# Splitting product 3 into seven small products in layers 0 to 4 of a cross network, with three of four state sums moved to accumulating DMAs

## The chip, the cores and the metric

The kernel runs on one core of a Trainium2 chip. The metric is the time of the device for one launch, in microseconds (us). A core has TensorE (PE in the profile; PEld are its weight loads, which overlap the products), VectorE (DVE), ScalarE (ACT), GpSimd (POOL), SyncE (SP, which here only starts DMAs) and 16 DMA engines that all queues share.

## The reference

```python
# x0: 16384 x 1024, ws: 6 x 1024 x 1024, bs: 6 x 1024, all bf16
x = x0
for l in range(6):
    proj = einsum('bd,de->be', x, ws[l]) + bs[l]
    x = x0 * proj + x
return x
```

## The kernel before, in words

The batch is cut into 16 pairs of 2 x 512 rows. A pair's state is held turned, features on the partitions: a tile `[128, 2, 8, 512]` with the two batch halves n and eight blocks of features. One pair in one layer is a 1024 x 1024 weight times 1024 rows, which Strassen's scheme (Winograd's form) makes of seven products of 512 x 512 by 512 rows, each 16 matmuls of 128 x 128 by 512. On the right sides of the products stand quarters of the state (products 1, 2 and 3) or differences of them made by VectorE: T13 (for products 5 and 7, one operation of 4096 elements a partition), T2 (product 6) and T4 (product 4). On the left stand quarters of the weight or combinations of them. ScalarE evicts the results from the accumulators (`ev`, with the bias where a sum is done, and `evi` for the small ones) into tiles P1s, P5s, S53, U2s and C2 (its pool is `cb`), and VectorE adds them up, multiplies by x0 and adds the state.

A product can itself be split once more: seven small products of 256 x 256 by 256 rows (`inner`, four matmuls of 128 x 128 by 256 each, line 429), in place of 16 matmuls in `mm` (line 421). This takes combined weights (`combo(l, 8)`, `(l, 9)`, `(l, 10)` for products 2, 4, 3), four differences of 512 elements of its right side (`inner_t`) and sums of its small results. Before the change product 2 is split everywhere but in the first step, product 4 from the second round on (`in4`), and product 3 in layer 0 alone from the second round on (`in3`), where the state's tile is still free to hold its differences and sums.

The loops: eight rounds `s`, each with two pairs, A and B; six layers `l`; and inside a layer the step of A, then that of B. So there are 96 steps, and A's next layer comes after B's step of this one. Each engine's queue is in the order in which the code writes it for VectorE, ScalarE, GpSimd and the DMA queues (`pin`). The step X first does what is left of the step before, Y: `trail(Y)` gives that as a list, m1 (product of C12 = S53 with x0), s11 (P5s into C2), a1 (adds the state), s4 and e4 (small sums of product 4), mC2 and aC2 (product and state sum of two quarters at once, 4096 elements). These are laid between X's T13, T2, T4 and the differences for the small products in the tuple `order` (line 464). Later in the step stand m0 and a0, the product and the state sum of the quarter that is ready first (`fin_of`), with j02, j1, j3, the differences for the next step's product 2; then the sum U2s into S53. C2 has two buffers.

In round 0 VectorE also makes the combined weights (`combo`), which are stored to `Lc` in HBM. Later rounds load nine weight tiles a layer into a ring of nine (`prefetch_upto`), all in SP's one queue: during B's step a tile of the next layer is loaded whenever one has had its last use. A tenth tile (product 3's combined weight, in buffer `P2s`) is loaded once a round, for layer 0. The next round's x0 is brought by four DMA transposes (`bring`, `load_x0`), two each in layers 2 and 3 of A. At a round's end the result is turned by a DMA transpose (`turn_pair`) and written (`write_pair`).

Of the kernel before, what the change touches and what calls it, by code (L numbers as in the profile page):

```python
# [17 lines left out]
def kernel(  # L18
# [14 lines left out]
    NB = 512  # L33
# [11 lines left out]
    def vtt(out, in0, in1, op):  # L45
        return pin(nc.vector.tensor_tensor(out=out, in0=in0, in1=in1, op=op))  # L46

    def vcopy(out, in_):
        return pin(nc.vector.tensor_copy(out=out, in_=in_))
# [7 lines left out]
    def pool(name, bufs, **kw):  # L57
        return ctx.enter_context(tc.tile_pool(name=name, bufs=bufs, **kw))
# [4 lines left out]
    t_pool, ti_pool, ei_pool = pool("tp", 1), pool("tip", 1), pool("eip", 1)  # L63
    ev_pool, cb_pool, wring = pool("evp", 1), pool("cbp", 2), pool("wring", RING)
    ps = [pool(f"ps{i}", KH, space=bass.MemoryType.PSUM) for i in range(2)]
# [192 lines left out]
    def trail(Y, store):  # L258

        if Y is None:  # L260
            return [None] * 7
        C2, E4, e5 = Y.C2, Y.E4, Y.e5
        eh1 = lambda t: t[:, :, KH:KD, :]
        m1, a1 = fin_of(Y, Y.C12, 0, 1)
        if Y.E3 is not None:
            def m1(E3=Y.E3, e6=Y.e6, C=Y.C12, mul=m1):
                for i in range(2):
                    vtt(E3[:, 2 * i:2 * i + 2, NQ:NB], E3[:, 2 * i:2 * i + 2, (1 - i) * NQ:(2 - i) * NQ], e6[:], ADD)
                vtt(C, C, E3, ADD)
                mul()  # L270

        def s4():
            for i in range(2):
                vtt(E4[:, 2 * i:2 * i + 2, NQ:NB], E4[:, 2 * i:2 * i + 2, (1 - i) * NQ:(2 - i) * NQ], e5[:], ADD)

        def a1s():
            if a1 is not None:
                a1()
            if store:
                store_half(Y, 0)  # L280

        return [m1, lambda: vtt(C2[:, 1], C2[:, 1], Y.P5s[:], ADD), a1s,
                s4 if E4 is not None else None,
                (lambda: vtt(C2[:, 0], C2[:, 0], E4[:], ADD)) if E4 is not None else None,
                lambda: vtt(eh1(Y.xst) if Y.l == 0 else C2[:], C2[:], eh1(Y.x0T), MULT),
                None if Y.l == 0 else (lambda: vtt(eh1(Y.xst), C2[:], eh1(Y.src_in), ADD))]

    def fin_of(Y, C, eh, n):
        xs = half(eh)
        if Y.l == 0:  # L290
            return [lambda: vtt(Y.xst[:, n, xs, :], C, Y.x0T[:, n, xs, :], MULT), None]
        return [lambda: vtt(C, C, Y.x0T[:, n, xs, :], MULT),
                lambda: vtt(Y.xst[:, n, xs, :], C, Y.src_in[:, n, xs, :], ADD)]
# [36 lines left out]
    def write_pair(Y):  # L330
        with nc.allow_non_contiguous_dma(reason="256B runs"):
            for n in range(2):
                r0 = Y.pr * PR + n * NB
                pin(nc.sync.dma_start(out[r0:r0 + NB, :].rearrange("(j p) (k r) -> p k j r", p=P, r=P),
                                      Y.x0T[:, n].rearrange("p k (j r) -> p k j r", r=P)))

    for s in range(NPAIR // 2):
        for l in range(L):
            for side in ("A", "B"):
                X, Y = cur[side], prev  # L340
                first, last = step == 0, (X.pr, l) == LAST
                in2, in4 = not first, s > 0 and not (s + 1 == NPAIR // 2 and l + 1 == L)
                X.l, in3 = l, l == 0 and s > 0
                psA, psX = ps[step % 2], ps[1 - step % 2]
# [12 lines left out]
                if side == "B" and s + 1 < NPAIR // 2 and l == L - 1:  # L357
                    w3i = evt("P2s")
                    pending.insert(0, lambda w=w3i: pin(nc.sync.dma_start(w[:], lc(0, 10))))
                if side == "A" and s + 1 < NPAIR // 2:  # L360
                    if l == (2 if s > 0 else L - 1):
                        pending.append(lambda: bring("A"))
                    if l == 3 and s > 0:
                        pending.append(lambda: bring("B"))

# [92 lines left out]
                i02, i1, i3 = inner_t(X, lambda: X.T[4], "ti4") if in4 else [None] * 3  # L458
                X.E3 = None
                k02, k1, k3 = [None] * 3  # L460
                if in3:
                    ti3 = X.xst[:, 0, KH:KD, :].rearrange("p q (k b) -> p q k b", k=2)
                    k02, k1, k3 = inner_t(X, lambda: X.rhs(3), "ti3", ti3)
                order = (m1, s11, a1, t2, k02, s4, k1, t4, k3, e4, i02, mC2, i1, aC2, i3)
                if in3 and side == "B":
                    order = (m1, s11, a1, t2, s4, t4, e4, k02, i02, k1, k3, mC2, i1, aC2, i3)
                for f in order:
                    if f is not None:
                        f()
                if in2:  # L470
# [23 lines left out]
                    mm(1, w1, pA, 3, True)  # L494
                    if last:
                        ev(P1s, pA, 3, 0)
# [23 lines left out]
                    if in3:  # L520
                        wk, wr3 = w3i[:].rearrange("p k (j e) -> p k j e", e=HE), sub_w(w3, HE)
                        b3, t3 = sub4(X.rhs(3)), X.ti3
                        colx = lambda m0, j, pX=pX: (lambda m: pX[m0 + m][:, j * NQ:(j + 1) * NQ])
                        inner(colx(0, 0), wr3[1, 0], b3[1, 0], False)
                        inner(colx(0, 1), wk[:, 2], b3[1, 1], False)
                        ev(S53, pX, 0, 0)
                        mm(5, w5, pX, 3, True)
                        ev(P5s, pX, 3)
                        ev(S53, pX, 1, 0)
                        ev(P1s, pA, 3, 0)  # L530
                    else:
                        mm(3, w3, pX, 0, False)
                        mm(5, w5, pX, 3, True)
                        ev(P5s, pX, 3)
                        ev(S53, pX, 0, 0)
                        if not last:
                            ev(P1s, pA, 3, 0)
                        for m in range(1, KH):
                            mm(3, w3, pX, m, False)
                            ev(S53, pX, m, 0)  # L540
# [55 lines left out]
                if last:  # L596
                    st00 = fin_rows(X, P1s[:], 0, 0)
                    fin_rows(X, P5s[:], 1, 1)
                for f in () if last else (m0, a0) if late else (j02, m0, j1, a0, j3):
                    if f is not None:  # L600
                        f()
                if s == 0:
                    if side == "A":
                        if l > 0 and l + 1 < L:
                            alloc(l + 1)
                        if l + 1 < L:
                            load_raw(l + 1, nc.sync, (12, 4, 1, 2) if l > 0 else (12,))
                        for pid in ((5, 6, 3) if 0 < l < L - 1 else ()):
                            combo(l + 1, pid)
                        if l in (0, L - 1):  # L610
                            combo(l, 9)
                    elif l + 1 < L:
                        for pid in (5, 6, 3) if l == 0 else ():
                            combo(1, pid)
                        combo(l + 1, 7)
                        combo(l + 1, 8)
                        if l == 0:
                            combo(0, 10)
                w6 = weights(6)
# [7 lines left out]
                if in4:  # L627
# [13 lines left out]
                    if in3:  # L641
                        y1, y5 = bank(psX), bank(psX)
                        X.E3 = X.xst[:, 1, 0:KH, :]
                        X.e6 = ei_pool.tile([P, 2, NQ], BF16, name="e6")
                        e3 = sub4(X.E3)
# [16 lines left out]
                    mm(6, w6, pA, 3, False)  # L662
                    ev(U2s, pA, 3)
                    if in3:
                        inner(cols(y1), wk[:, 1], t3[:, 1], False)
                        evi(e3[0, 1], y1)
                    mm(7, w7, pA, 0, False)
                    ev(C2[:, 1], pA, 0, 1)
                    inner(cols(z1), wj[:, 3], t4[:, 2], False)
                    evi(e4[1, 0], z1)  # L670
                    for m in range(1, KH):
                        mm(7, w7, pA, m, False)
                        ev(C2[:, 1], pA, m, 1)
                        if in3 and m == 1:
                            inner(cols(y1), wk[:, 3], t3[:, 2], False)
                            evi(e3[1, 0], y1)
                    col = lambda m0, j, pA=pA: (lambda m: pA[m0 + m][:, j * NQ:(j + 1) * NQ])
# [12 lines left out]
                else:  # L690
# [11 lines left out]
                if s == 0 and side == "B" and 0 < l < L - 1:  # L702
                    combo(l, 9)
                if not last:
                    vtt(S53[:], U2s[:], S53[:], ADD)
                if late:
                    for f in (j02, j1, j3):
                        if f is not None:
                            f()
# [49 lines left out]
```

## Time and profile before

| | us |
|---|---|
| median of three runs (lowest, highest) | 2262.54 (2261.4, 2265.69) |
| the profiled execution | 2261.87 |
| its span in the profile | 2260.1 |
| TensorE, VectorE, ScalarE, GpSimd busy in it | 2239.8, 2140.5, 1929.8, 1.6 |
| DMA moved | 338.82 MB, mean 150 GB/s |

The span is what the profile covers; some 1.8 us lie around it. An engine's busy time is the union of its instructions' times, so where one begins before the last has ended the overlap counts once. The granted clock of TensorE is 1.00 in every stretch that is used here. Shares of the DMA engines are means over 16 of them.

### The profile page before, as it was taken

Reading aid. Unit: us, or ns where it says so; the run is one execution under the profiler, and the core shown is the slowest. Engines: PE = TensorE matmul, PEld = TensorE weight load, DVE = VectorE, ACT = ScalarE, POOL = GpSimd, SP = SyncE. Lnnn points to the kernel's source line nnn. Section 1 sums busy time; section 2 is a strip of 40 time slices with the busy share of each in tenths; the row PEclk is TensorE's granted clock in tenths of the full one; section 3 lists DMA queues with packets and bytes.
Section 4 is the critical chain, followed back from the end, with each engine's and each line's share of the span. In section 5 each row is a group of like instructions: output and inputs, shape, how many; then the busy total and the mean of one; then the engine's idle time right before and its main releaser. Section 6 shows DMA issues by size and latency. Waiting matters only on the chain.

```text
span 2260.1 us, 33725 instructions
## 1 busy us (share of the span) xinstructions
PE 2239.8 (99%) x12838; PEld 1279.2 (57%) x13093; DVE 2140.5 (95%) x2445; ACT 1929.8 (85%) x3363; POOL 1.6 (0%) x10
## 2 busy tenths in 40 slices
PE   9999999999999999999999999999999999999999
PEld 4555555555655556555565555655556555565554
DVE  7999989999999999999999999999999999999999
ACT  7777788888988889888898888988889888898887
POOL 0000000000000000000000000000000000000000
PEclk9999999999999999999999999999999999999999
DMA  8423595523945249543494434944348443583337
GB/s 245 146 94 121 160 213 167 141 85 131 256 131 136 94 131 259 132 122 101 134 260 122 122 114 135 246 122 122 125 134 235 121 131 122 137 227 122 105 120 177
DMA packets 509638, 338.82 MB, mean 150 GB/s; under 512 B 390690, under 2 KB 470564, under 8 KB 509476
## 3 DMA queue, kind: packets, MB, share of 16 engines
q1 hardware_dynamic: 509412, 336.63, 53.2%
q8 instruction: 103, 1.69, 0.3%
q14 instruction: 59, 0.48, 0.1%
q10 hardware_dynamic: 64, 0.01, 0.0%
HBM read 217.59 MB, written 52.95 MB: 120 GB/s over the span
## 4 chain that ended last, share of the span: by engine, by line
PE 99%; issue 1%; DMA 0%; DVE 0%; ACT 0%
PE px L421 72%; PE px L429 26%; PE px L416 1%; DMA b_rows<-in_bs_dram 0%; DVE cb L46 0%; PE px L228 0%; PE px L413 0%; PE px L411 0%; ACT cb L52 0%; ACT big L52 0%; DVE zero L200 0%; PE px L234 0%; PE px L243 0%
## 5 line engine op out<-in xcount | busy, mean ns | idle before, releaser
L421 PE MATMUL px<-T,wp 128*128 128x512 bf16 x4255 | 1058.4, 379 | 6.5
L421 PEld LDWEIGHTS <-wp 128*128 128x128 bf16 x7120 | 696.4, 98 | 637.0 <-DMA wp<-in_ws_dram 0.4
L421 PE MATMUL px<-big,wp 128*128 128x512 bf16 x2627 | 645.4, 379 | 6.0 <-DMA wp<-in_ws_dram 0.2
L429 PEld LDWEIGHTS <-wp 128*128 128x128 bf16 x4920 | 480.9, 98 | 257.4 <-DVE big L46 2.8
L55 ACT ACTIVATE cb<-px,b_all 128x512 bf16<-128x512 f32 x760 | 504.5, 689 | 78.4 <-PE px L421 64.9
L429 PE MATMUL px<-ti,wp 128*128 128x256 bf16 x2684 | 402.7, 273 | 0.1
L52 ACT CAST ea<-px 128x512 bf16<-128x512 f32 x344 | 201.7, 586 | 133.6 <-PE px L429 133.6
L46 DVE TENSOR_TENSOR T<-big 128x4096 bf16<-128x4096 bf16 (+2 forms) x98 | 220.3, 2248 | 78.0 <-PE px L421 77.1
L52 ACT CAST U2s<-px 128x512 bf16<-128x512 f32 x384 | 229.2, 597 | 55.3 <-PE px L421 52.8
L55 ACT ACTIVATE P1s<-px,b_all 128x512 bf16<-128x512 f32 x376 | 251.4, 694 | 4.2 <-PE px L421 2.7
L55 ACT ACTIVATE S<-px,b_all 128x512 bf16<-128x512 f32 x380 | 244.1, 703 | 0.6 <-PE px L421 0.5
L46 DVE TENSOR_TENSOR T<-big,T 128x2048 bf16<-128x2048 bf16 x192 | 234.4, 1221 | 1.6 <-PE px L429 0.5
L52 ACT CAST P5s<-px 128x512 bf16<-128x512 f32 x384 | 219.2, 596 | 15.7 <-PE px L421 14.5
L46 DVE TENSOR_TENSOR big<-cb,big 128x4096 bf16<-128x4096 bf16 x95 | 217.6, 2291 | 0.4
L52 ACT CAST e<-px 128x512 bf16<-128x512 f32 x342 | 204.4, 606 | 0.0
L429 PE MATMUL px<-big,wp 128*128 128x256 bf16 x1252 | 187.9, 273 | 0.0
L46 DVE TENSOR_TENSOR cb<-cb,big 128x4096 bf16<-128x4096 bf16 (+2 forms) x89 | 185.4, 2086 | 0.7 <-ACT cb L52 0.5
L52 ACT CAST eb<-px 128x512 bf16<-128x512 f32 x258 | 152.1, 590 | 6.2
L429 PE MATMUL px<-T,wp 128*128 128x256 bf16 x984 | 134.2, 273 | 0.1
L46 DVE TENSOR_TENSOR S<-U2s,S 128x2048 bf16<-128x2048 bf16 (+1 forms) x97 | 117.4, 1210 | 3.1 <-ACT U2s L52 3.0
L46 DVE TENSOR_TENSOR P1s<-P1s,big 128x2048 bf16<-128x2048 bf16 x90 | 109.9, 1221 | 7.9 <-ACT P1s L55 7.8
L46 DVE TENSOR_TENSOR cb<-cb,P5s 128x2048 bf16<-128x2048 bf16 (+1 forms) x97 | 117.2, 1208 | 0.1
(81 smaller groups left out, 1479.9 us busy)
## 6 DMA issues: line engine op xcount, KB each, us to landing
wp<-Lc SPq DMA_DIRECT2D x252, 512.0 KB, 4.6
wp<-in_ws_dram SPq DMA_DIRECT2D x144, 512.0 KB, 3.5
out_dram<-big SPq DMA_DIRECT2D x28, 1024.0 KB, 10.8
Lc<-big SPq DMA_DIRECT2D x15, 512.0 KB, 2.7
Lc<-wp SPq DMA_DIRECT2D x9, 512.0 KB, 2.7
Lc<-ti SPq DMA_DIRECT2D x7, 512.0 KB, 3.7
P2s<-Lc SPq DMA_DIRECT2D x7, 512.0 KB, 4.2
ea<-in_ws_dram SPq DMA_DIRECT2D x6, 512.0 KB, 4.9
```

The costliest lines, as they stand in the source:

```text
L46: return pin(nc.vector.tensor_tensor(out=out, in0=in0, in1=in1, op=op))
L52: return pin(nc.scalar.copy(out=out, in_=in_))
L55: return pin(nc.scalar.activation(out=out, in_=in_, func=IDENT, bias=bias, scale=1.0))
L416: nc.tensor.matmul(pt, lhsT=rhs[:, k, m * P:(m + 1) * P], rhs=wt[:, k, :], start=(start and k == 0 and pid != 1), stop=(k == KH - 1), **kw)
L421: nc.tensor.matmul(pts[m][:], lhsT=wt[:, k, m * P:(m + 1) * P], rhs=rhs[:, k, :], start=(start and k == 0), stop=(k == KH - 1), **kw)
L429: nc.tensor.matmul(dst(m), lhsT=w[:, k, m * P:(m + 1) * P], rhs=rhs[:, k, :], start=(start and m == 0 and k == 0), stop=(k == 1), skip_gro ...
```

## The change

Product 3 is split in layers 0 to 4 of rounds 1 to 7 (`in3`), with its sums added to S53 in the step itself, in a tile E3 of its own (`e3`), and its differences in a tile `ti3`. Its combined weight is made in round 0 for each of these layers (`combo(l, 10)`) and loaded once a layer (`load_third`). The order in which VectorE's and ScalarE's work is written is new, and the same for A and B.

In the steps for which `by_dma` holds (layers 1 to 4 of A, 1 to 3 of B, in all rounds) three of the four state sums are no longer VectorE's: the product with x0 goes into a tile (T2's buffer, U2s, or a quarter of C2), and a DMA started by GpSimd adds that tile, 512 KB, to the state in place (`dadd`). The fourth quarter is still summed by VectorE. C2 has one buffer. The x0 of the next round is brought in layer 5 of A.

```diff
+    def dadd(out, in_):
+
+        pin(nc.gpsimd.dma_start(out=out, in_=in_, accum_op=ADD))
...
-    ev_pool, cb_pool, wring = pool("evp", 1), pool("cbp", 2), pool("wring", RING)
+    ev_pool, cb_pool, wring = pool("evp", 1), pool("cbp", 1), pool("wring", RING)
...
+        dma = by_dma(Y)
+        mul = lambda n: vtt(C2[:, n], C2[:, n], Y.x0T[:, n, KH:KD, :], MULT)
...
+        def m1d():
+            vtt(Y.U2s[:], Y.C12, Y.x0T[:, 1, 0:KH, :], MULT)
+            dadd(Y.xst[:, 1, 0:KH, :], Y.U2s[:])
+
+        def m2d():
+            mul(1)
+            dadd(Y.xst[:, 1, KH:KD, :], C2[:, 1])
+
+        s11 = lambda: vtt(C2[:, 1], C2[:, 1], Y.P5s[:], ADD)
...
+        if dma:
+            return [m1d, s11, m2d, s4, e4, lambda: mul(0),
+                    lambda: vtt(Y.xst[:, 0, KH:KD, :], Y.xst[:, 0, KH:KD, :], C2[:, 0], ADD)]
...
+    def by_dma(Y):
+        return 0 < Y.l < L - 1 - Y.pr % 2
 
     def fin_of(Y, C, eh, n):
...
+        if by_dma(Y):
+            def m0():
+                t = t_pool.tile([P, KH, NB], BF16, name="T2")
+                vtt(t[:], C, Y.x0T[:, n, xs, :], MULT)
+                dadd(Y.xst[:, n, xs, :], t[:])
+
+            return [m0, None]
...
+    def load_third(l):
+        third[l] = evt("P2s")
+        pin(nc.sync.dma_start(third[l][:], lc(l, 10)))
...
-                X.l, in3 = l, l == 0 and s > 0
+                X.l, in3 = l, s > 0 and l < L - 1
...
-                    if l == (2 if s > 0 else L - 1):
+                    if l == L - 1:
                         pending.append(lambda: bring("A"))
-                    if l == 3 and s > 0:
-                        pending.append(lambda: bring("B"))
+                        if s > 0:
+                            pending.append(lambda: bring("B"))
...
-                order = (m1, s11, a1, t2, k02, s4, k1, t4, k3, e4, i02, mC2, i1, aC2, i3)
-                if in3 and side == "B":
-                    order = (m1, s11, a1, t2, s4, t4, e4, k02, i02, k1, k3, mC2, i1, aC2, i3)
+                order = (m1, s11, k02, a1, k1, t2, k3, t4, s4, i02, e4, i1, mC2, i3, aC2) if in3 else (m1, s11, a1, t2, s4, t4, e4, i02, mC2, i1, aC2, i3)
...
-                for f in () if last else (m0, a0) if late else (j02, m0, j1, a0, j3):
+                for f in () if last else (m0, a0) if late else (j02, m0) if in3 else (j02, m0, j1, a0, j3):
...
-                        if l in (0, L - 1):
-                            combo(l, 9)
+                        combo(l, 9)
...
-                        if l == 0:
-                            combo(0, 10)
+                        combo(l, 10)
...
-                        X.E3 = X.xst[:, 1, 0:KH, :]
+                        X.E3 = ei_pool.tile([P, KH, NB], BF16, name="e3")
...
-                    inner(cols(z1), wj[:, 3], t4[:, 2], False)
-                    evi(e4[1, 0], z1)
+                    if in3:
+                        inner(cols(y1), wk[:, 3], t3[:, 2], False)
+                        evi(e3[1, 0], y1)
+                        if side == "B" and l + 1 < L - 1:
+                            load_third(l + 1)
+                    else:
+                        inner(cols(z1), wj[:, 3], t4[:, 2], False)
+                        evi(e4[1, 0], z1)
...
                 if not last:
                     vtt(S53[:], U2s[:], S53[:], ADD)
+                if in3:
+                    e3sum = lambda i: vtt(X.E3[:, 2 * i:2 * i + 2, NQ:NB], X.E3[:, 2 * i:2 * i + 2, (1 - i) * NQ:(2 - i) * NQ], X.e6[:], ADD)
+                    js = () if late else (j1, a0, j3)
+                    for f in js[:2] + (lambda: e3sum(0),) + js[2:]:
+                        if f is not None:
+                            f()
+                    e3sum(1)
+                    vtt(S53[:], S53[:], X.E3[:], ADD)
```

More of the change, by code (lines that the diff above doesn't have):

```diff
@@ L263, in trail @@
         eh1 = lambda t: t[:, :, KH:KD, :]
[L264 to L270, printed above, removed]
+        dma = by_dma(Y)
+        mul = lambda n: vtt(C2[:, n], C2[:, n], Y.x0T[:, n, KH:KD, :], MULT)
         def s4():
@@ L274, in s4 @@
                 vtt(E4[:, 2 * i:2 * i + 2, NQ:NB], E4[:, 2 * i:2 * i + 2, (1 - i) * NQ:(2 - i) * NQ], e5[:], ADD)
+        def m1d():
[5 more added lines that the diff above has]
+        s11 = lambda: vtt(C2[:, 1], C2[:, 1], Y.P5s[:], ADD)
+        e4 = (lambda: vtt(C2[:, 0], C2[:, 0], E4[:], ADD)) if E4 is not None else None
+        if E4 is None:
+            s4 = None
+        if dma:
+            return [m1d, s11, m2d, s4, e4, lambda: mul(0),
+                    lambda: vtt(Y.xst[:, 0, KH:KD, :], Y.xst[:, 0, KH:KD, :], C2[:, 0], ADD)]
+        m1, a1 = fin_of(Y, Y.C12, 0, 1)
         def a1s():
@@ L280, in a1s @@
                 store_half(Y, 0)
-        return [m1, lambda: vtt(C2[:, 1], C2[:, 1], Y.P5s[:], ADD), a1s,
-                s4 if E4 is not None else None,
-                (lambda: vtt(C2[:, 0], C2[:, 0], E4[:], ADD)) if E4 is not None else None,
+        return [m1, s11, a1s, s4, e4,
                 lambda: vtt(eh1(Y.xst) if Y.l == 0 else C2[:], C2[:], eh1(Y.x0T), MULT),
                 None if Y.l == 0 else (lambda: vtt(eh1(Y.xst), C2[:], eh1(Y.src_in), ADD))]
+    def by_dma(Y):
+        return 0 < Y.l < L - 1 - Y.pr % 2
     def fin_of(Y, C, eh, n):
@@ L335, in write_pair @@
                                       Y.x0T[:, n].rearrange("p k (j r) -> p k j r", r=P)))
+    third = {}
+    def load_third(l):
+        third[l] = evt("P2s")
+        pin(nc.sync.dma_start(third[l][:], lc(l, 10)))
     for s in range(NPAIR // 2):
@@ L357 @@
                 if side == "B" and s + 1 < NPAIR // 2 and l == L - 1:
-                    w3i = evt("P2s")
-                    pending.insert(0, lambda w=w3i: pin(nc.sync.dma_start(w[:], lc(0, 10))))
+                    pending.insert(0, lambda: load_third(0))
                 if side == "A" and s + 1 < NPAIR // 2:
-                    if l == (2 if s > 0 else L - 1):
+                    if l == L - 1:
                         pending.append(lambda: bring("A"))
-                    if l == 3 and s > 0:
-                        pending.append(lambda: bring("B"))
+                        if s > 0:
+                            pending.append(lambda: bring("B"))
                 if s + 1 == NPAIR // 2 and side == "A" and l == 2:
@@ L458 @@
                 i02, i1, i3 = inner_t(X, lambda: X.T[4], "ti4") if in4 else [None] * 3
-                X.E3 = None
                 k02, k1, k3 = [None] * 3
                 if in3:
-                    ti3 = X.xst[:, 0, KH:KD, :].rearrange("p q (k b) -> p q k b", k=2)
-                    k02, k1, k3 = inner_t(X, lambda: X.rhs(3), "ti3", ti3)
-                order = (m1, s11, a1, t2, k02, s4, k1, t4, k3, e4, i02, mC2, i1, aC2, i3)
-                if in3 and side == "B":
-                    order = (m1, s11, a1, t2, s4, t4, e4, k02, i02, k1, k3, mC2, i1, aC2, i3)
+                    k02, k1, k3 = inner_t(X, lambda: X.rhs(3), "ti3")
+                order = (m1, s11, k02, a1, k1, t2, k3, t4, s4, i02, e4, i1, mC2, i3, aC2) if in3 else (m1, s11, a1, t2, s4, t4, e4, i02, mC2, i1, aC2, i3)
                 for f in order:
@@ L494 @@
                     mm(1, w1, pA, 3, True)
-                    if last:
+                    if last or in3:
                         ev(P1s, pA, 3, 0)
@@ L520 @@
                     if in3:
-                        wk, wr3 = w3i[:].rearrange("p k (j e) -> p k j e", e=HE), sub_w(w3, HE)
+                        wk, wr3 = third[l][:].rearrange("p k (j e) -> p k j e", e=HE), sub_w(w3, HE)
                         b3, t3 = sub4(X.rhs(3)), X.ti3
@@ L529 @@
                         ev(S53, pX, 1, 0)
-                        ev(P1s, pA, 3, 0)
                     else:
@@ L662 @@
                     mm(6, w6, pA, 3, False)
-                    ev(U2s, pA, 3)
                     if in3:
@@ L666 @@
                         evi(e3[0, 1], y1)
+                    ev(U2s, pA, 3)
                     mm(7, w7, pA, 0, False)
                     ev(C2[:, 1], pA, 0, 1)
-                    inner(cols(z1), wj[:, 3], t4[:, 2], False)
-                    evi(e4[1, 0], z1)
+                    if in3:
[6 more added lines that the diff above has]
+                        evi(e4[1, 0], z1)
                     for m in range(1, KH):
@@ L674 @@
                         if in3 and m == 1:
-                            inner(cols(y1), wk[:, 3], t3[:, 2], False)
-                            evi(e3[1, 0], y1)
+                            inner(cols(z1), wj[:, 3], t4[:, 2], False)
+                            evi(e4[1, 0], z1)
                     col = lambda m0, j, pA=pA: (lambda m: pA[m0 + m][:, j * NQ:(j + 1) * NQ])
@@ L701 @@
                         ev(C2[:, 0], pA, m, 1)
-                if s == 0 and side == "B" and 0 < l < L - 1:
-                    combo(l, 9)
+                X.U2s = U2s
                 if not last:
                     vtt(S53[:], U2s[:], S53[:], ADD)
+                if in3:
[6 more added lines that the diff above has]
+                    vtt(S53[:], S53[:], X.E3[:], ADD)
                 if late:
```

## The prediction

> **What bounds the kernel now.** I read the page first: engine shares and the chain that ended last.
>
> ```profile
> PE 2239.8 (99%) x12838; PEld 1279.2 (57%) x13093; DVE 2140.5 (95%) x2445; ACT 1929.8 (85%) x3363; POOL 1.6 (0%) x10
> ...
> PE 99%; issue 1%; DMA 0%; DVE 0%; ACT 0%
> ```
>
> TensorE is busy throughout and is the whole chain; GpSimd does nothing. VectorE at 95% comes next, so a change that gives it work must be counted there. A mean over stages hides what one step costs, so I then cut round 3 into steps: the windows run from one step's first P1s eviction to the next one's. The rows are, of round 3, layer 3 A, layer 4 A, layer 4 B, layer 0 A and layer 0 B, and layer 2 B of round 0.
>
> ```profile
> 995.05:1018.43 23.38, 23.22 (x135) 13.30 (x137) 22.43 (x26) 20.10 (x37) 0.00 (x0) 1.00 0.60 132
> 1041.81:1065.19 23.38, 23.22 (x135) 13.30 (x137) 22.43 (x26) 20.10 (x37) 0.00 (x0) 1.00 0.11 44
> 1065.19:1088.57 23.38, 23.22 (x135) 13.31 (x137) 22.43 (x26) 20.10 (x37) 0.00 (x0) 1.00 0.50 164
> 855.47:878.46 22.99, 22.89 (x148) 14.48 (x149) 22.70 (x31) 21.45 (x41) 0.00 (x0) 1.00 1.13 265
> 878.46:901.53 23.07, 22.91 (x147) 14.39 (x149) 21.56 (x30) 21.47 (x41) 0.00 (x0) 1.00 0.96 258
> 128.44:152.22 23.78, 23.62 (x123) 12.14 (x125) 22.96 (x27) 18.67 (x32) 0.00 (x0) 1.00 0.21 76
> ```
>
> After the length come busy TensorE, weight loads, VectorE, ScalarE and GpSimd, then granted clock, DMA share and GB/s. Round 0 splits one product into seven (23.78 us), layers 1 to 5 of later rounds split products 2 and 4 (23.38), layer 0 there splits product 3 too (22.99 in A). Each split saves 0.40, even in a step where ScalarE is busy 21.45 and VectorE 22.70 of 22.99: TensorE still sets the length. The matmul groups agree: 8 in 1.89 us give a pitch of 0.216, 4 small ones in 0.60 a pitch of 0.109; 16 x 0.216 - 28 x 0.109 = 0.40.
>
> For VectorE I use the pitch from start to start, since durations overlap:
>
> ```profile
> 1010.31 1.22 DVE L46 TENSOR_TENSOR P1s<-P1s,big 128x2048 bf16<-128x2048 bf16 x1
> 1011.45 0.42 DVE L46 TENSOR_TENSOR ti<-big,ti 128x512 bf16<-128x512 bf16 x1
> 1011.78 1.22 DVE L46 TENSOR_TENSOR big<-P1s,big 128x2048 bf16<-128x2048 bf16 x1
> ...
> 1015.32 2.29 DVE L46 TENSOR_TENSOR T<-big 128x4096 bf16<-128x4096 bf16 x1 [0.84 <-PE px L421]
> 1017.52 1.22 DVE L46 TENSOR_TENSOR S<-S,big 128x2048 bf16<-128x2048 bf16 x1
> ```
>
> So 2048 elements cost 1.135 us, 512 cost 0.335, 4096 cost 2.20 (and 1024 0.60 by the rows before these). The bracket is VectorE's spare time: at each step T13 waits 0.84 us for TensorE.
>
> **The change, part by part.**
>
> Product 3 split: rounds 1 to 7, layers 1 to 4, two sides, 56 steps x 0.40 = 22.4 us less for TensorE.
>
> Its order: layer 0 B is 0.09 longer than A. The waits have the weight load of a small product waiting 2.8 us in 7 times for VectorE's "big", the differences of product 3, which B now makes late. The new order makes them early in both sides: 7 x 0.09 = 0.6 us.
>
> ScalarE: four more casts a step at a pitch of 0.48. Layer 0 carries them today (21.45 of 22.99): free.
>
> VectorE, middle layers. Before: 3 x 2.20 + 10 x 1.135 + 0.60 + 11 x 0.335 = 22.24 of 23.38. Out: the sums a0 and a1 (2 x 1.135) and half of the 4096-wide sum (the product beside it is only cut in two); in: four differences and two e3 sums of 512, one sum of 2048. Now 1 x 2.20 + 12 x 1.135 + 0.60 + 17 x 0.335 = 22.12 of 22.98. It fits with 0.86 us to spare; without the DMAs it would be 22.24 + 6 x 0.335 + 1.135 = 25.4 and the bound. One step overflows, layer 0 A: its sums on E3 move from the next step into its own, and the full trail of layer 5 falls there too; 22.45 + 1.81 = 24.26, 1.3 late. Layer 0 B takes 20.92 and wins it back. In between T13 ends 3.2 us into the step while product 5 first reads it at 5.2: hidden. Layer 4 B (not by DMA) has 23.25, 0.3 late, given back in layer 5.
>
> A new wait of VectorE: product m0 now goes into a T2 buffer, of which there is one, and product 6 reads the old content. By the matmul pitches product 6 ends 17.5 us into a step; VectorE is there at 16.7 and waits 0.8. Behind it stand the U2s sum, which waits for product 6's evictions anyway (19.1), the last differences for the next product 2 and the e3 sums, which end at 22.8; the next T13 could start at 22.3. It starts 0.5 late against 3 or more of room, and with this lag the wait shrinks: nothing. In round 0 the wait is longer (12.2 to 17.1), but these steps lose 3.27 us of VectorE's work; with the two combos that are added or moved T13 ends at most 3.2 us into the next step, again ahead of 5.2. Nothing.
>
> One cb buffer instead of two: the next eviction into it comes 18 us into a step; its last reader, the one sum left on VectorE, ends at 14 (14.7 plus the lag in layer 0 A). Hidden; were that cover gone, TensorE would stop for evictions.
>
> The accumulating DMAs: 56 steps x 3 = 168, 512 KB each, from GpSimd. No trace here shows one. Occupancy: layer 4's steps move nine loads of 512 KB at shares of 0.11 and 0.50, so one load holds all 16 engines for 0.61 x 23.38 / 9 = 1.58 us. That is the low end. The high end: the transpose of 2 MB inside SBUF lands in 12.8 us, 3.2 per 512 KB, and twice that for two operands, 6.4. I take 2 x 1.58 = 3.2: a sum has two operands to bring in, and a contiguous copy of 4 KB rows is nearer to the load than to a transpose. Two steps then need 10 x 1.58 + 6 x 3.2 = 35 of 46 us: DMA is not the bound. Landing: 2.7 to 4.9 us in the rows of 512 KB, so I expect 4 to 7. Who waits: X.T2 for the DMA that empties the T2 buffer, 10.7 us after it is issued; U2s' next eviction, 9 us; C2's, 12 us; the state's next reader T13, 16 us. GpSimd's queue holds nothing else. All are covered; where a landing takes over 10 us, VectorE's 0.86 goes first, then TensorE waits.
>
> SP's queue: product 3's second weight tile is now loaded once a layer. It goes out behind the load that waits for a B step's last matmul, about 0.6 us into the next step; needed 9.5 us in. Loads at such a boundary land in 3.4 to 4.7 us today, 6.4 in layer 0. Room 2 to 4 us: nothing, but thin. The four x0 transposes move together to layer 5 A. Two of them cost layer 3 A 0.60 - 0.11 = 0.49 of a step's engines, so four fill layer 5 A (0.10 today) and spill a few us into layer 5 B; the weights that B loads have most of a step of room. Round 0's combos: above.
>
> A rule speaks against this. The trace shows GpSimd beside VectorE only in the last round, where its memsets (0.31 us the largest) run under a product of 1.22 us, unlengthened. The Trainium skill, SBUF — State Buffer, section "SBUF: two separate sides", warns that GpSimd writes the descriptors of its DMAs itself, is locked out while VectorE runs in a two-port mode, and that such a DMA should go to another queue. By that page's "Who interferes with whom" a two-input operation takes only the read side, so the sum would not move; no run here shows it.
>
> Sum: 22.4 + 0.6 = 23.0. The profiled execution took 2261.87 (span 2260.1, 1.8 around it), so 2238.9; the median of the three runs is 0.7 above it, so 2239.5.
>
> **The rivals.**
>
> Late landings. The T2 buffer or the second weight tile comes late by a few tenths to a microsecond at the 28 step boundaries where that tile joins three loads and accumulations. For: the thin room above, landings of 6 to 7.6 us in layer 0. Against: no wait of TensorE for a weight today in the steady rounds. 28 x 0.5 = 14 us back: 2253; range 2245 to 2258.
>
> The DMA engines become the bound (slower). Place: steps with three accumulations beside the loads of two steps. Price: two steps take 15.8 + 6a; at a = 6.4 that is 54.2, 27.1 a step, 3.7 over today's, in 49 steps of rounds 1 to 7: some +180, 2440. It decides from a = (46.8 - 15.8) / 6 = 5.2. For: the transpose's row. Against: the load's row, and plain 4 KB rows.
>
> GpSimd and VectorE hold each other up (slower). If each issue blocks VectorE for its length x, a middle step takes 22.12 + 3x; over today's 23.38 from x = 0.42. At x = 1 it is 25.1: 49 x 1.7 = 85, 2345. Against: the memset rows. The skill's rule above would be this case if it held for operations of two inputs.
>
> The change could also cancel: landings late by just 0.8 a boundary give 2262.
>
> **How the numbers follow.** Forecast as summed 0.58; late landings, still faster, 0.17; cancel 0.03; DMA-bound 0.13; port 0.09. Faster by over 0.2% (4.5 us, about what can be told from no change here): 0.75; same 0.03; slower 0.22. The range starts at 2234 (a few more lost tenths of today's steps) and reaches over late landings and no change to 2268, which leaves about 0.2 out.
>
> **What would show it.** Right: middle steps of 22.98; VectorE some 22.1 busy by pitch, T13 starting with no or a short idle; 168 transfers on a new GpSimd queue, landing in under 9 us; DMA share about 0.5 in A and 0.9 in B steps. Wrong: TensorE or its weight loads waiting for the P2s tile, VectorE's T idle with a DMA as releaser, two-input rows longer than 1.22, or steps longer than 23.38 with the DMA share at 1.

## The result and the profile after

The changed kernel takes 2239.99 us (median of five runs, 2239.35 to 2241.76); the kernel before took 2261.93 on the same chip (five runs, 2261.26 to 2265.69). The ratio is 0.9902, with a 95% interval of 0.9888 to 0.9916: 22 us faster, where 23.0 were forecast. The profiled execution took 2241.76 (span 2240.0) and is the slowest of the five. In one experiment, e5_layer5, two of six runs, the profiled one among them, lie over 1.5% above the fastest and are left out of its ratio.

From the page after: the engines' shares, the new DMA queue (packets, MB, share of 16 engines) and the chain that ended last.

```profile
PE 2217.2 (99%) x13503; PEld 1346.1 (60%) x13765; DVE 2145.2 (96%) x2797; ACT 2013.8 (90%) x3587; POOL 146.2 (7%) x178
q0 software_dynamic: 24192, 88.09, 21.7%
PE 96%; DVE 2%; DMA 1%; issue 1%; SPq 0%; ACT 0%; DVEq 0%; ACTq 0%
```

TensorE lost 22.6 us of busy time and is still the chain, but for the end: from 2181 us on the chain runs through VectorE, some 56 us of it, which is the 2% above. VectorE's busy time hardly moved although seven-product sums were added in 28 more steps a side. The new queue q0 holds the 168 accumulating DMAs of 512 KB (88 MB).

The windows of the changed kernel, cut in the same way as before: of round 3, layer 4 A and layer 0 B; then layer 2 B of round 0, and layer 1 A of round 1. The columns are length, busy TensorE, weight loads, VectorE, ScalarE, GpSimd, granted clock, DMA share, GB/s.

```profile
1034.99:1057.97 22.98, 22.82 (x147) 14.47 (x149) 22.49 (x32) 21.57 (x40) 2.58 (x3) 1.00 0.53 138
874.11:897.09 22.98, 22.82 (x147) 14.48 (x149) 22.28 (x31) 21.57 (x40) 0.00 (x0) 1.00 0.98 258
129.89:153.67 23.78, 23.62 (x123) 12.15 (x125) 21.44 (x28) 18.66 (x32) 2.58 (x3) 1.00 0.58 156
343.18:366.89 23.71, 23.00 (x147) 14.40 (x149) 21.29 (x30) 21.68 (x41) 0.86 (x1) 1.00 0.47 158
```

All of these lengths but the last were forecast: 23.38 has become 22.98 in the middle layers, layer 0 B has lost its 0.09, round 0 stays at 23.78 with GpSimd's DMAs in it. Of the 56 steps in which the split is new, 55 take 22.98 or 22.99; the last row is the odd one, 0.73 us too long. Three GpSimd instructions in 2.58 us are the issues of three DMAs, 0.86 us each.

VectorE's timeline at the boundary that the prediction looked at, layer 3 A into layer 3 B:

```profile
1005.68 1.23 DVE L46 TENSOR_TENSOR S<-U2s,S 128x2048 bf16<-128x2048 bf16 x1 [0.32 <-ACT U2s L56]
...
1008.28 1.23 DVE L46 TENSOR_TENSOR S<-S,e 128x2048 bf16<-128x2048 bf16 x1
1009.42 2.29 DVE L46 TENSOR_TENSOR T<-big 128x4096 bf16<-128x4096 bf16 x1
```

Before, T13 (the 4096-wide row) stood behind 0.84 us of waiting for TensorE. Now it starts without a bracket, straight behind the last e3 sum, and TensorE does not wait for it. What VectorE has left to spare has moved ahead of the U2s sum (0.32 in the bracket).

The DMA issues (out<-in, count, KB each, median us from issue to landing):

```profile
big<-T POOLq DMA_DIRECT2D x56, 512.0 KB, 5.0
big<-U2s POOLq DMA_DIRECT2D x56, 512.0 KB, 5.6
big<-cb POOLq DMA_DIRECT2D x56, 512.0 KB, 7.7
P2s<-Lc SPq DMA_DIRECT2D x35, 512.0 KB, 6.7
```

### The profile page after: what moved, and what is told of

It reads as the page before. It is cut to its first block, busy times and chain, and to the rows that moved or that the text cites. A ratio compares the mean times of both kernels' runs of the same rounds, so it can differ in the third digit from the quotient of the medians.

```text
span 2240.0 us, 36436 instructions
## 1 busy us (share of the span) xinstructions
PE 2217.2 (99%) x13503; PEld 1346.1 (60%) x13765; DVE 2145.2 (96%) x2797; ACT 2013.8 (90%) x3587; POOL 146.2 (7%) x178
## 3 DMA queue, kind: packets, MB, share of 16 engines
q0 software_dynamic: 24192, 88.09, 21.7%
## 4 chain that ended last, share of the span: by engine, by line
PE 96%; DVE 2%; DMA 1%; issue 1%; SPq 0%; ACT 0%; DVEq 0%; ACTq 0%
PE px L450 62%; PE px L458 33%; DVE cb L46 1%; DMA P2s<-Lc 0%; DVE big L46 0%; DVE S L46 0%; DVE T L46 0%; DMA b_rows<-in_bs_dram 0%; DVE P1s L46 0%; PE px L232 0%; DVE P5s L46 0%; DVE ti L46 0%; DVE ea L46 0%; DVE e L46 0%; PE px L238 0%
## 5 line engine op out<-in xcount | busy, mean ns | idle before, releaser
L450 PEld LDWEIGHTS <-wp 128*128 128x128 bf16 x6224 | 608.9, 98 | 507.3 <-issue 0.6
L458 PEld LDWEIGHTS <-wp 128*128 128x128 bf16 x5592 | 547.2, 98 | 263.8
L458 PE MATMUL px<-ti,wp 128*128 128x256 bf16 x2964 | 444.7, 273 | 0.1
L450 PE MATMUL px<-big,wp 128*128 128x512 bf16 x1759 | 440.4, 379 | 4.4
L56 ACT CAST e<-px 128x512 bf16<-128x512 f32 x608 | 352.5, 618 | 19.1 <-PE px L458 19.1
L59 ACT ACTIVATE P1s<-px,b_all 128x512 bf16<-128x512 f32 x376 | 243.3, 696 | 4.2 <-PE px L450 2.7
L458 PE MATMUL px<-big,wp 128*128 128x256 bf16 x1644 | 246.6, 273 | 0.0
L46 DVE TENSOR_TENSOR T<-big,T 128x2048 bf16<-128x2048 bf16 x192 | 234.5, 1222 | 1.2
L46 DVE TENSOR_TENSOR cb<-cb,big 128x2048 bf16<-128x2048 bf16 (+3 forms) x145 | 194.1, 1340 | 0.4
L50 POOL DMA_DIRECT2D big<-T x56 | 48.3, 863 | 1508.6 <-DVE T L46 1508.6
L46 DVE TENSOR_TENSOR ti<-big,ti 128x512 bf16<-128x512 bf16 x332 | 139.7, 421 | 0.4
L458 PEld LDWEIGHTS <-P2s 128*128 128x128 bf16 x1120 | 109.5, 98 | 43.4 <-DMA P2s<-Lc 0.8
```

Source lines behind the costliest of these rows:

```text
L50: pin(nc.gpsimd.dma_start(out=out, in_=in_, accum_op=ADD))
L56: return pin(nc.scalar.copy(out=out, in_=in_))
L59: return pin(nc.scalar.activation(out=out, in_=in_, func=IDENT, bias=bias, scale=1.0))
L450: nc.tensor.matmul(pts[m][:], lhsT=wt[:, k, m * P:(m + 1) * P], rhs=rhs[:, k, :], start=(start and k == 0), stop=(k == KH - 1), **kw)
L458: nc.tensor.matmul(dst(m), lhsT=w[:, k, m * P:(m + 1) * P], rhs=rhs[:, k, :], start=(start and m == 0 and k == 0), stop=(k == 1), skip_gro ...
```

## The experiments

Every kernel is the changed one with the edit shown. "Ratio" is to the kernel before, measured beside it, with its 95% interval.

**The split with VectorE's sums, without the DMAs** (e1_no_dma).

```diff
-        return 0 < Y.l < L - 1 - Y.pr % 2
+        return False
```

> All four state sums stay on VectorE (by_dma is never true); product 3 stays split. My theory: VectorE becomes the bound in the middle layers. By its pitches a middle step is 22.24 + 6 x 0.335 + 1.135 = 25.4 us against 22.98 of TensorE, 7 such steps a round, 16.9 us too much a round, of which some 4 to 5 us can be carried as lag and given back in layers 5, 0 and 1: about 12 us lost in each of 7 rounds, so 2240 + 85 = 2325 (2300 to 2345), slower than the kernel before; GpSimd's queue empty. Rival, that VectorE has room over a whole round (267 us of work by pitch in 276.6 of TensorE) and the DMAs are not needed: 2240 to 2245.

Measured: 2363.52, ratio 1.0447 (1.0431 to 1.0463). The window of layer 4 A of round 3:

```profile
1077.56:1103.28 25.72, 23.81 (x151) 14.30 (x149) 25.58 (x33) 21.21 (x40) 0.00 (x0) 1.00 0.12 49
```

VectorE becomes the bound, as worked out: 25.58 busy of 25.72. The split alone, without a place for the sums, costs 101 us. The size was missed by 39. By start-to-start pitches the step has 25.39 of work, and some 0.33 of small gaps that the sum left out. Seven such steps a round are 7 x 2.74 = 19.2 us longer than TensorE's 22.98, and a round lost 17.1 (round 3: 293.6 against 276.6): the lighter steps took back about 2.1 us of a late VectorE, not the 4 to 5 assumed.

**The DMAs without the split** (e2_no_split).

```diff
-                X.l, in3 = l, s > 0 and l < L - 1
+                X.l, in3 = l, s > 0 and l == 0
...
-                        if side == "B" and l + 1 < L - 1:
+                        if False:
                             load_third(l + 1)
```

> The 168 accumulating DMAs stay, product 3 is split in layer 0 alone as before the change. My theory: the DMAs cost TensorE nothing, so the time is the old one less 0.6 us for layer 0's order: 2261 to 2262, middle steps 23.38 long, VectorE waiting some 3.5 us a step. Rival, that the DMAs take time from TensorE through late buffers, through the port that GpSimd and VectorE share or through late weights: 2265 or more, with steps over 23.38.

Measured: 2261.19, ratio 0.9995 (0.9986 to 1.0004). Layer 4 A of round 3:

```profile
1041.36:1064.74 23.38, 23.38 (x138) 13.30 (x137) 19.44 (x25) 20.09 (x37) 2.58 (x3) 1.00 0.49 120
```

The step keeps the length that it had before the change, with VectorE at 19.44 busy and 168 accumulating DMAs beside it. So these DMAs cost nothing that can be measured, and they buy nothing by themselves either. The 21.2 us from here to the changed kernel are the split: step by step it is the 0.40 forecast, 22.4 in all, less the one odd step and what a start and an end vary by (below).

**More for the DMA engines to do** (e3_copies1, e3_copies2). Behind each accumulating DMA, GpSimd copies the same 512 KB once or twice to a place in HBM that nobody reads (the diff is of e3_copies1; e3_copies2 has `range(2)`).

```diff
+        for _ in range(1):
+            pin(nc.gpsimd.dma_start(out=extra_dst[count[0] % 12].rearrange("p (k e) -> p k e", k=KH), in_=in_))
+            count[0] += 1
...
```

> Behind each accumulating DMA GpSimd starts one plain DMA of the same 512 KB to a scratch tensor in HBM that nobody reads. My theory: what counts is how long the 16 engines are held; the accumulation holds them 2.9 us (21.7% of 2240 us over 168), a copy about 1.6 by the row of loads, 4.5 in all, and two steps then need 10 x 1.58 + 6 x 4.5 = 43 of 46 us: still under the bound of 5.0, so 2240 to 2252, the DMA share over 0.9 in the B steps. Rival, that landing times decide (the T2 buffer is released by the copy's landing, 10.7 us after its issue at the latest): T2 late in many steps, 2260 or more already here.

> The same with two plain copies behind each accumulating DMA. My theory: 2.9 + 2 x 1.6 = 6.1 us for each, so two steps need 10 x 1.58 + 6 x 6.1 = 52 of 46 us; the DMA engines become the bound, about 26 us a step, 49 x 3.1 = 150 more: 2390 (2330 to 2440), TensorE waiting for weights and VectorE for T2. Rival, that DMAs in flight overlap so far that shares over 1 are possible (layer 0 shows 1.09): 2240 to 2260.

Measured: 2245.07 with one copy, ratio 0.9924 (0.991 to 0.9937), and 2444.8 with two, ratio 1.0806 (1.0786 to 1.0826). With one copy, layer 4 B of round 3 still takes 22.98 us, at a DMA share of 0.84. With two, layer 4 A takes 35.31; TensorE's wait for the P2s tile (us in total, times, longest):

```profile
PE px L463 <- DMA P2s<-Lc: 132.1, 22, 10.3
```

From the queue's shares, an accumulation holds the 16 engines for 21.7% x 2240 / 168 = 2.89 us, and a copy for (31.3% x 2243.2 - 21.7% x 2240) / 168 = 1.29 with one, 1.28 a copy with two. By the prediction's sum two steps then take 15.8 + 6 x 4.18 = 40.9 of 46 us with one copy, which costs 5 us in the whole kernel, and 15.8 + 6 x 5.45 = 48.5 with two, which costs 205. The steep edge lies between 4.2 and 5.45, where the rival put it (5.2). But the loss isn't spread over all steps: it lies in the A steps of layers 2 to 4 (29.7, 31.0 and 35.3 in round 3), where TensorE waits 6 us on average, and up to 10, for the one tile P2s, issued last and needed first. The 2444.8 are just beyond the 2330 to 2440 expected.

**The same two copies, with the P2s tile queued earlier** (e7_copies2_first).

```diff
-                    w4, w4i, w7 = weights(4), weights(9), weights(7)
+                    w4 = weights(4)
+                    if in3 and side == "B":
+                        w4i, w7 = W[s, l, 9], W[s, l, 7]
+                    else:
+                        w4i, w7 = weights(9), weights(7)
...
-                        if side == "B" and l + 1 < L - 1:
-                            load_third(l + 1)
+                        if side == "B":
+                            if l + 1 < L - 1:
+                                load_third(l + 1)
+                            prefetch_upto(pos[s, l, 7] + RING)
```

> The two plain copies behind each accumulating DMA as in the run before, but product 3's weight tile is put into SP's queue as soon as its buffer is free, ahead of the two loads that wait for the end of B's step. Theory one, from the run before (its steps of 30 to 35 us are all A's, and TensorE waits there for the P2s tile): the first thing to give way is this one load at the step boundary, not the sum of the DMA engines' work; with some 9 us more room for it most of the 200 us come back: 2245 to 2280. Theory two, my prediction's: the engines are simply full (by the runs 10 x 1.58 + 6 x (2.89 + 2 x 1.28) = 48.5 us in 46), and another load or the T2 buffer is late instead: 2320 to 2450.

Measured: 2392.11, ratio 1.0579 (1.0563 to 1.0595). Two of the waits (us in total, times, longest), and the windows of layers 3 A and 3 B of round 3:

```profile
ACT U2s L59 <- DMA extra_dst<-U2s: 93.4, 25, 5.0
PE px L463 <- DMA wp<-in_ws_dram: 65.6, 21, 5.3
```
```profile
1055.86:1084.58 28.72, 23.47 (x150) 14.30 (x149) 22.57 (x32) 21.99 (x40) 5.88 (x9) 1.00 0.89 287
1084.58:1107.57 22.99, 22.99 (x150) 14.48 (x149) 22.50 (x32) 21.22 (x41) 5.83 (x9) 1.00 0.94 289
```

The wait for P2s is gone, 53 us came back, and the rest moved to the next late transfers: the buffers that the copies read, and the weights. The two steps of layer 3 hold the engines for 0.89 x 28.72 + 0.94 x 22.99 = 47 us, more than the 46 that they had: as the prediction's sum has it, there is more to move than time. The order in the queue was worth 53 us of the 205 and decided who waited. That the A steps take nearly all of the loss isn't explained.

**The early P2s tile alone** (e6_third_first): the edit just above, without the copies.

> Nothing added; product 3's weight tile is put into SP's queue as soon as its buffer is free, ahead of the two loads that wait for the end of B's step. My theory: the one late load of the changed kernel (0.71 us in layer 1 of A in round 1) goes, and nothing else changes, since all other boundaries have room: 2239.0 to 2240, landing of the tile some 9 us ahead of its use. Rival, that other steps lose time at this boundary which the releasers do not show: 2237 or less.

Measured: 2240.17, ratio 0.9902 (0.9889 to 0.9915): no different from the changed kernel. In its trace round 1's layer 1 A takes 22.98 and nothing waits for P2s. The thin room costs one wait of 0.7 us in the changed kernel's profiled execution, too little for the median to show.

**No wait for the T2 buffer** (e4_m0_in_place): the product m0 is written over P1s and added to the state from there.

```diff
-                t = t_pool.tile([P, KH, NB], BF16, name="T2")
-                vtt(t[:], C, Y.x0T[:, n, xs, :], MULT)
-                dadd(Y.xst[:, n, xs, :], t[:])
+                vtt(C, C, Y.x0T[:, n, xs, :], MULT)
+                dadd(Y.xst[:, n, xs, :], C)
```

> The product m0 is written over P1s and added from there, so that VectorE no longer waits for product 6 to leave the T2 buffer; instead the next step's first eviction into P1s waits for the DMA's landing. My theory: the wait for T2 costs nothing now, in the middle layers or in round 0, so nothing is won: 2239 to 2241.5; P1s is needed 24.4 us after the step's start, the DMA lands at about 17.9 + 5 = 23, so a landing over 6.5 us would show as a wait of ScalarE. Rival, that the wait for T2 does hold back VectorE and with it TensorE somewhere: 2237 or less.

Measured: 2240.7, ratio 0.9905 (0.9892 to 0.9918): the wait that the change added to VectorE costs nothing.

**The split in layer 5 as well** (e5_layer5), in rounds 1 to 6, with the sums of layers 4 B and 5 by DMA too and the early P2s tile. By the split's price this should have been worth some 12 x 0.40 more.

```diff
-        return 0 < Y.l < L - 1 - Y.pr % 2
+        return 0 < Y.l and not (Y.l == L - 1 and Y.pr // 2 == NPAIR // 2 - 1)
...
-                X.l, in3 = l, s > 0 and l < L - 1
+                X.l, in3 = l, s > 0 and (l < L - 1 or s + 1 < NPAIR // 2)
...
```

> Product 3 is split in layer 5 of rounds 1 to 6 too, with the weight tile loaded early as in the kernel beside it, and three of four state sums go by DMA in layer 4 of B and layer 5 as well (not in the last round). My theory: 12 more steps fall from 23.38 to 22.98, 4.8 us: 2235 (2234 to 2237), if the landings beside the transposes of layers 5 and 0 stay covered (DMA shares there are 1.0 to 1.1 already, a product quarter's DMA has 10.7 us). Rival, that layers 5 and 0 have no DMA time left: T2, the turned result or weights late, some 3 us or more a round, 2240 to 2270.

Measured: 2598.98 (median of six, 2569.56 to 2640.18), ratio 1.1434 (1.1391 to 1.1477). Both expectations fell. Nearly all long steps are layer 5 A and layer 0 A, the ones in which x0 comes in through DMA transposes and the result is turned by others. Layer 5 A of round 1 takes 44.34 us; its DMA issues:

```profile
big<-U2s POOLq DMA_DIRECT2D x1, 512.0 KB, 30.2
big<-in_x_dram SPq DMA_TRANSPOSE x4, 13.7
```

The accumulations from U2s and from cb, beside the transposes, land after 30 us. In the changed kernel's trace none of the 168 accumulations is under way together with a transpose, since the x0 transposes have left layers 2 and 3. The prediction charged that move nothing, for another reason. The next two runs put the transposes back.

**The x0 transposes back in layers 2 and 3** (e8_bring_23), everything else as changed.

```diff
-                    if l == L - 1:
+                    if l == (2 if s > 0 else L - 1):
                         pending.append(lambda: bring("A"))
-                        if s > 0:
-                            pending.append(lambda: bring("B"))
+                    if l == 3 and s > 0:
+                        pending.append(lambda: bring("B"))
```

> The changed kernel, but the x0 transposes of the next round are brought in layers 2 and 3 of A again, as before the change: they now run beside the accumulating DMAs of those steps. Theory, from the run with layer 5 added (a transpose there held SP's queue 23 us and landed after 35, the accumulations beside it after 30): each pair of transposes delays the accumulations by some 20 us, U2s' and C2's evictions wait, and the weight loads behind the transposes are late; some 15 us in each of two steps in 6 rounds: 2240 + 180 = 2420 (2320 to 2520). Rival, that only the sum of the engines' shares counts: 0.60 + 0.41 is about one step's worth and its neighbours have room, 2240 to 2246.

Measured: 2509.95, ratio 1.1081 (1.1051 to 1.1111). Twelve steps, layers 2 A and 3 A of rounds 1 to 6, take 42 to 53 us in place of 22.98; in the profiled executions they hold 293 us more, and the whole time is 292 longer. Round 1, layer 3 A (48.54 us): SP's queue (start, us), and the DMA issues, the two transposes one by one.

```profile
463.09 35.02 SPq L224 DMA_TRANSPOSE big<-in_x_dram  x1
498.16 5.78 SPq L224 DMA_TRANSPOSE big<-in_x_dram  x1
```
```profile
big<-U2s POOLq DMA_DIRECT2D x1, 512.0 KB, 33.4
big<-cb POOLq DMA_DIRECT2D x1, 512.0 KB, 33.2
big<-in_x_dram SPq DMA_TRANSPOSE x1, 39.3
big<-in_x_dram SPq DMA_TRANSPOSE x1, 9.2
```

The same two transposes in the same place of the kernel before:

```profile
434.76 7.82 SPq L220 DMA_TRANSPOSE big<-in_x_dram  x1
442.94 4.13 SPq L220 DMA_TRANSPOSE big<-in_x_dram  x1
```

There they landed after 10.5 and 6.2 us. Now the first holds SP's queue for 35.02 us and lands after 39.3, and the accumulations beside it land four to six times as late as without it (33 for 5.6 and 7.7). The second is issued when they have all but landed and takes little longer than before. While the first and the accumulations overlap, the DMA engines show a share of 0.9 or more and move mostly 20 to 90 GB/s; the transposes of the kernel before moved some 290. The wait that this makes (us in total, times, longest):

```profile
ACT U2s L56 <- DMA big<-U2s: 274.3, 12, 28.1
```

Twelve times 23 us on average: ScalarE can't evict into U2s until the DMA has read it. That is most of the 292.

**The same with plain copies** (e9_bring_23_copy): as e8, and GpSimd's DMAs copy over the state in place of adding to it, so the addition is left out of the computation.

```diff
-        pin(nc.gpsimd.dma_start(out=out, in_=in_, accum_op=ADD))
+        pin(nc.gpsimd.dma_start(out=out, in_=in_))
```

> As the run before it, but GpSimd's 168 DMAs copy the product over the state where they added to it; the addition of the state is left out with that, its place, size and queue are kept. If it is the adding that goes badly beside a transpose, this one is undisturbed: 2240 to 2246. If any DMA from GpSimd's queue does it, it is as slow as the one with the addition, 2320 to 2520. In between, the delay goes with the DMA's own work: a copy has one operand to bring in, about half.

Measured: 2347.15, ratio 1.0392 (1.0353 to 1.0431). In the same place (round 1, layer 3 A), the issues beside the first transpose:

```profile
big<-U2s POOLq DMA_DIRECT2D x1, 512.0 KB, 13.5
big<-cb POOLq DMA_DIRECT2D x1, 512.0 KB, 18.0
big<-in_x_dram SPq DMA_TRANSPOSE x1, 23.7
```

A plain copy beside a transpose is held up too: over the whole run the medians of the three tiles are 3.2, 4.1 and 4.5. ScalarE's wait for U2s falls from 274.3 to 88.6 us. So the conflict isn't one of the addition alone. With the addition the kernel loses 2.5 times as much, counted from the changed one, (2509.95 - 2239.99) / (2347.15 - 2239.99); that is the "about half" of the last expectation, though 2347 lies in the range of the one before it as well. What inside the DMA engines makes the two kinds slow each other stays open: these runs change only who meets whom. Nor do they tell GpSimd's queue from the path, SBUF to SBUF, since no run sends such copies through SP's queue.

## Why the prediction was right, point by point

**The split, 56 x 0.40.** Right: 55 of the 56 steps went from 23.38 to 22.98, and e2 isolates the term at 21.2 us. **The order, 0.6.** Right: layer 0 B is 22.98, in e2 as well, where nothing else is split.

**VectorE, 22.12 of 22.98.** Right, and it was the step that all depended on: from one T13 to the next the pitches of layers 2 to 4 add up to 22.12. The 0.86 to spare are in the trace too, but not in front of T13, which waited 77.1 us for TensorE before the change. After it, the idle time ahead of T13, ahead of m0 (T<-P1s) and ahead of the U2s sum:

```profile
L46 DVE TENSOR_TENSOR T<-big 128x4096 bf16<-128x4096 bf16 x95 | 217.1, 2286 | 2.4 <-PE px L450 1.6
L46 DVE TENSOR_TENSOR T<-P1s,big 128x2048 bf16<-128x2048 bf16 x56 | 68.6, 1225 | 26.3 <-PE px L450 24.8
DVE S L46 <- ACT U2s L56: 26.1, 64, 3.2
```

Of the 0.86 a step, 0.33 are the small gaps that e1 shows as well, where VectorE waits for nobody; 0.41 are the wait for U2s' evictions and 0.12 the wait for the T2 buffer. So about half a microsecond a step is left. The two steps that were to run over did so and were hidden: T13 comes 1.1 us later than elsewhere behind layer 0 A (1.3 forecast) and behind 4 B (0.3 forecast, too little).

**What it would cost without the DMAs.** 25.4 was the right sum of pitches, 0.33 short of a real step; e1's 2363.52 shows what VectorE as the bound costs. In the forecast the 0.33 were covered by the 0.86 to spare.

**The T2 wait and the single cb buffer.** Right at nothing. The wait for T2 is the 24.8 us of the second row: 2.0 to 2.4 us a time in round 0 (4.9 forecast), 1.24 in layer 1 A of most later rounds and 0.12 in layers 2 to 4 (0.8 forecast, to shrink). e4 without it is no faster.

**Occupancy and landing.** 3.2 us forecast, 2.89 measured, between bounds of 1.6 and 6.4. The reason given, two operands to bring in, fits: a plain copy of the same tile takes a little less than half (below). Landing was forecast at 4 to 7: 5.0 and 5.6 fit, 7.7 for cb is mis-sized, within its room of 12 us.

**The boundary of the P2s tile.** "Nothing, but thin" was right. Loads at a boundary were taken at 3.4 to 4.7 us; this one took 6.7 (median), up to 9.9. It mostly lands 2 to 3 us ahead of its use; in layer 1 A of round 4 it was 0.06 us, and in round 1 the 9.9 us cost a step 0.73. e6 takes that away for no measurable gain; e3_copies2 shows that it is the first thing to break. So the rival of late landings had the right place, and its 0.5 us at 28 boundaries was one wait.

**GpSimd and VectorE.** The rival's condition never arose: the two-input row is 1222 ns with 168 issues beside it, 1221 before, and each issue took 0.86 us under a VectorE that was 96% busy.

**Moving the four x0 transposes.** Right at nothing, and by luck in part. The step weighed engine shares and found room in layer 5 A, rightly (a share of 1.15 there in round 3, and the step still takes 23.38); it didn't ask what a transpose does to the accumulations that now stand in layers 2 and 3. Had the transposes stayed there, the change would have been 248 us slower than before (e8), not 22 faster. The move isn't a free companion of the change but a condition for it, and so is the end of the accumulations ahead of layer 5 (e5). No rival held this case.

**The sum.** 22 of 23.0. The profiled execution lies 2.9 above its forecast of 2238.9: round 0 ended 1.45 later (296.33 against 294.88), the late P2s tile 0.7, the end 0.55. The median of five shows less of it, 0.5 above the forecast.

## What to carry to other kernels

When the second engine has no room for the work that relieves the first, count the second by start-to-start pitches, step by step, and move whole sums off it: here a transfer that adds in place was free as long as its landing had room, it met no transpose, and two steps' transfers together stayed well under the steps' length. Ask of each transfer that is added or moved not only how much of the DMA engines it takes but which kind it meets there: in these runs keeping transposes and GpSimd-queued transfers apart in time was worth more than ten times the change itself. Queue first the load that has least room before its use, since here that one failed first.

## What the runs showed of the hardware

A DMA transpose and a 512 KB transfer from GpSimd's queue, accumulating or plain, slow each other when they run together from early on: in e8 and e9 (round 1, layer 3 A) the transfers land after 33 us with the addition and 13.5 to 18 without, the transpose after 39.3 and 23.7, where apart they take 3 to 8 (medians) and 10.5. With the addition the engines move mostly a third or less of the bytes per second, at a DMA share near 1. An overlap at the end alone did no harm: ten accumulations of e8 that began 1 to 3 us before a transpose landed took 4.5 to 5.7 us. The Trainium skill, DMA: Bandwidth & Descriptors, section "Rules for kernel authors", says that a transpose next to ordinary DMAs needs nothing; that may hold for what it computes, but not for the time in this case.

An accumulating DMA of 512 KB holds the 16 engines 2.89 us on average. The plain copy between the same tiles takes about half where no transpose is near: in layer 4 A of round 3 GpSimd's queue has a share of 35.0% in the changed kernel and 16.7% in e9, over three transfers in 22.98 us, which is 2.68 us against 1.28.

After a wait of 10 us TensorE was slow on top of it. TensorE's timeline in e3_copies2 behind the wait for P2s, and the windows right behind it and 6 us on (the figure before the DMA share is the granted clock):

```profile
1140.01 1.03 PE L463 MATMUL px<-big,P2s 128*128 128x256 bf16 x4 [10.32 <-DMA P2s<-Lc]
1140.84 3.47 PE L455 MATMUL px<-T,wp 128*128 128x512 bf16 x8
```
```profile
1140.00:1144.00 4.00, 3.99 (x12) 1.79 (x13) 0.00 (x0) 1.86 (x3) 0.00 (x0) 0.50 0.32 130
1146.00:1150.00 4.00, 4.00 (x30) 2.74 (x28) 0.44 (x1) 3.73 (x9) 0.00 (x0) 1.00 0.02 4
```

Eight matmuls take 3.47 us in place of 1.89 while the granted clock stands at 0.50. Each of the 21 waits of 5 us or more in that run was followed by 2.8 to 6.0 us of this; at half speed that is 1.4 to 3.0 us lost on top of the wait, an estimate from these figures. The Trainium skill, TensorE: Matmul & The Clock Gate, section "What's actually happening", has the clock at half after an idle window of about 3.4 us and back after as long a busy one; the trace agrees for these waits. But three waits of 2.1 to 2.7 us in round 0 of the same run, shorter than that window, were followed by half the clock as well, for 3.41 us each.
